# A third pass of seven half-size products in the first of two MLPs, on one Trainium2 core

## The chip, the core and the metric

The kernel runs on one core of a Trainium2 chip. The metric is device time of one execution in microseconds; the kernel before takes 1666.81 us, the median of three runs (1665.36 to 1667.01). Engines in the rows: PE is the matrix engine (TensorE), PEld its weight loads, DVE the vector engine, ACT the activation engine, POOL GpSimd, SP the queue that issues all DMAs here.

## What is computed

Attention over pooled keys and values for 8 batches of 576 tokens with 8 heads of 64, then two MLPs of 512 x 2048 x 512 over all 4608 tokens:

```python
def _attn_ref(q, k, v):                      # [8, 8, 576, 64]
    k_p = k.reshape(B, H, Sp, 8, D).mean(axis=3)
    v_p = v.reshape(B, H, Sp, 8, D).mean(axis=3)
    scores = scale * np.matmul(q, k_p.transpose(0, 1, 3, 2))
    ...                                      # softmax over 72 pooled keys
    return np.matmul(attn, v_p)
def _moe_ref(x, w_in, w_out):                # 4608 x 512, 512 x 2048, 2048 x 512
    h = x @ w_in
    return np.maximum(0.01 * h, h) @ w_out
def _moe2_ref(x, w_in, w_out):
    r = np.maximum(x @ w_in, 0.0)
    return (r * r) @ w_out
```

The weights arrive as 64-bit floats, which the kernel turns into 32-bit ones itself ("decoding").

## The kernel before

Every product in 32-bit precision is made of three matmuls (`three`, lines 271 to 276): each operand is split into a rounded part `hi` and a rest `lo` (a cast on ACT, a subtraction on DVE), and hi hi, hi lo and lo hi are accumulated.

The first MLP treats its 4608 tokens in two ways. The first 3072 go in six **plain tiles** of 512 tokens. A unit is one tile `t` and one 128-wide slice `f` of the 2048 hidden columns (16 to a tile): `first` makes 12 matmuls into `h`, applies the leaky ramp and splits the result into `gh` and `gl`; `second` makes 12 matmuls into four accumulators. The weights stay in SBUF in full and are split again for each unit by `split_weights` (two casts and two subtractions of 128 x 512). The remaining 1536 tokens go in two **passes** of 768 (`LEAD` = 2): `first2` and `second2` compute a 2 x 2 block product with seven half-size products in place of eight, with blocks of 384 tokens (`HT`). A pass is 56 steps ("hooks") of 12 matmuls of 384 columns; each needs one weight block of 512 KB, loaded from DRAM by `next_block` through a ring of six buffers, five of them ahead. The second MLP is six passes of the same make over all tokens, whose `second2` has 18 matmuls of 256 columns a hook.

The blocks of the first MLP come from two places: the plain halves are stored by `split_weights` in tile `NTILE - 2` (line 190) and the sums of halves by `prepare_sums`. The blocks of the second MLP come from `prepare_products` (lines 237 to 269): for each of 8 slice pairs and for `in` and `out` it loads 1 MB, decodes, forms four sums, splits all into `hl` (one buffer) and stores 768 KB and 1 MB. It is a generator; each `next` is a step, 8 steps for an `in` block and 9 for an `out` block, 136 in all.

Order: everything is traced in the order of the loop at line 908, and the framework then orders each engine's instructions by that order and by readiness. The loop hands out attention steps (`advance`: 3 a unit in tile 0, 5 later, `RATES`), then one step of `prepare_sums` a unit, and once attention is through, three steps of `prepare_products` a unit (line 941). In the second half of the last tile the pools of the passes are opened over the space of the early weights (lines 944 to 956) and `products_x(0)` splits the operands of the first pass, one of seven a unit. In the passes (line 972) every second hook is given one step of `prepare_products` until they are used up. Stores are put off by some ticks (`later`, `tick`) so that SP does not wait for the data.

Of the kernel before, what the change touches and what calls it, by code (L numbers as in the profile page):

```python
# [8 lines left out]
F32 = mybir.dt.float32  # L9
F32R = mybir.dt.float32r  # L10
# [7 lines left out]
P = 128  # L18
POOL = 8
KM = 64  # L20
TT = 512
# [6 lines left out]
def raw(ap):  # L28

    return ap.bitcast(F32)  # L30
# [3 lines left out]
def attention_two_mlps(  # L34
# [12 lines left out]
    B, H, S, D = q.shape  # L47
    NT, DM = out.shape
# [10 lines left out]
    AHEAD = 5  # L59
    RATES = (3, 5)  # L60
    HT = 384
    NTILE = 6
    NPASS = NT // (2 * HT)
    PLAIN = NTILE * TT
    LEAD = (NT - PLAIN) // (2 * HT)
    NQ = NF // 2
    HD = DM // 2
    RING = 6
# [3 lines left out]
    dpool = ctx.enter_context(tc.tile_pool(name="dram", bufs=1, space=DRAM))  # L72
# [3 lines left out]
    xpool = one_stack.enter_context(tc.tile_pool(name="x", bufs=5))  # L76
    gpool = one_stack.enter_context(tc.tile_pool(name="g", bufs=2))
# [4 lines left out]
    ps_a = one_stack.enter_context(tc.tile_pool(name="ps_a", bufs=4, space=PSUM))  # L82
# [4 lines left out]
    def temp(name, dt=F32):  # L87
        return tpool.tile([P, TT], dt, tag="t", name=name)

    def work(name, n=TT, early=False):  # L90
        if early:
            return ps_a.tile([P, n], F32, tag="acc", name=name)
        return ps_w.tile([P, n], F32, tag="w", name=name)
# [5 lines left out]
    nc.scalar.activation(warm, ident[:, 0:1], AF.Exp)  # L99


    x0 = [dpool.tile([DM, TT], F32, name=f"x0_{t}") for t in range(NTILE)]
    x0 += [dpool.tile([DM, HT], F32, name=f"x0_{NTILE + t}") for t in range(2 * LEAD)]
    x1 = [dpool.tile([DM, HT], F32, name=f"x1_{t}") for t in range(NT // HT)]

# [5 lines left out]
    def place(g):  # L111

        if g < PLAIN:
            return g // TT, g % TT, TT
        return NTILE + (g - PLAIN) // HT, (g - PLAIN) % HT, HT


# [3 lines left out]
    def later(n, **kw):  # L121
        LATE.append([n, kw])
# [59 lines left out]
    def split_weights(kind, t, f):  # L182

        w = W[kind, f]
        hl = hlpool.tile([P, 2, TT], F32R, tag="hl", name=f"hl_{kind}_{t}_{f}")
        hi, lo = hl[:, 0], hl[:, 1]
        nc.scalar.copy(hi, w)
        nc.vector.tensor_tensor(out=lo, in0=w, in1=raw(hi), op=ALU.subtract)  # L188
        HL[kind, t, f] = (hi, lo)
        if t == NTILE - 2:  # L190
            p, i = f % NQ, f // NQ
            for j in range(2):
                part = {(0, 0): 0, (0, 1): 1, (1, 1): 2}.get((i, j) if kind == "in" else (j, i))
                if part is not None:
                    later(
                        2, out=WD[1, kind, p // 2][part, :, p % 2].rearrange("p (h x) -> p h x", h=2),
                        in_=raw(hl)[:, :, j * HD:(j + 1) * HD],
                    )
# [404 lines left out]
    ready = [0]  # L603
# [10 lines left out]

    def new_x(t):
        X[1, t] = [
            tuple(xpool.tile([P, TT], F32R, tag=g, name=f"{g}1_{t}_{c}") for g in ("xh", "xl"))
            for c in range(NK)
        ]

    def load_x(t):
        XS[t] = []
        for c in range(NK):
            st = temp(f"xs1_{t}_{c}")
            nc.sync.dma_start(out=st, in_=x0[t][c * P:(c + 1) * P, :])
            XS[t].append(st)

# [9 lines left out]
    def first(t, f):  # L637

        x = X[1, t]
        wh, wl = HL.pop(("in", t, f))  # L640
        h = work(f"h1_{t}_{f}")
        for c in range(NK):
            cs = slice(c * P, (c + 1) * P)
            three(h, (wh[:, cs], wl[:, cs]), x[c], c == 0, c == NK - 1)
        g = temp(f"g1_{t}_{f}")
        nc.scalar.activation(g, h, AF.Prelu, alpha=0.01)
        gh = gpool.tile([P, TT], F32R, tag="gh", name=f"gh1_{t}_{f}")
        gl = gpool.tile([P, TT], F32R, tag="gl", name=f"gl1_{t}_{f}")
        nc.scalar.copy(gh, g)  # L649
        nc.vector.tensor_tensor(out=gl, in0=g, in1=raw(gh), op=ALU.subtract)  # L650
        G[t, f] = (gh, gl)

    A = {}

    def store_x1(t, j, o):
        at = t * TT
        while at < (t + 1) * TT:
            n = min((t + 1) * TT, (at // HT + 1) * HT) - at
            nc.sync.dma_start(
                out=x1[at // HT][j * P:(j + 1) * P, at % HT:at % HT + n], in_=o[:, at - t * TT:at - t * TT + n]  # L660
            )
            at += n

    def second(t, f):
        gh, gl = G.pop((t, f))
        wh, wl = HL.pop(("out", t, f))
        if f == 0:
            A[t] = [ps_a.tile([P, TT], F32, tag="acc", name=f"acc1_{t}_{j}") for j in range(4)]
        acc = A[t]
        for j in range(4):  # L670
            js = slice(j * P, (j + 1) * P)
            three(acc[j], (wh[:, js], wl[:, js]), (gh, gl), f == 0, f == NF - 1)
        if f == NF - 1:
            for j in range(4):
                o = temp(f"o1_{t}_{j}")
                if j % 2 == 0:
                    nc.scalar.copy(o, acc[j])
                else:
                    nc.vector.tensor_copy(o, acc[j])
                store_x1(t, j, o)  # L680
# [6 lines left out]
    def load_x2(t):  # L687
        XS2[t] = []
        for j in range(2):
            src = x0[NTILE + 2 * t + j] if t < LEAD else x1[2 * (t - LEAD) + j]  # L690
            st = x2pool.tile([P, NK, HT], F32, tag=f"xs{j}", name=f"xs2_{t}_{j}")
# [10 lines left out]
    def products_x(t):  # L702
# [21 lines left out]
    uses = [  # L724
        (1 if t < LEAD else 2, kind, a, prod)
        for t in range(LEAD + NPASS)
        for kind, a, prod in [("in", a, o[1]) for a in range(NQ // 2) for o in ORDER]
# [81 lines left out]
    def second2(t):  # L809
        banks = {}  # L810
        shape = [P, 2, HT] if t < LEAD else [P, 3, HD]
        s1, s2, s5 = (tmpool.tile(shape, F32, tag=f"s{i}", name=f"so{i}_{t}") for i in (1, 2, 5))
        stores = []
        xg = products_x(t + 1) if t + 1 < LEAD + NPASS else iter(())
        for k, (i, prod) in enumerate(ORDER):
# [35 lines left out]
            else:  # L851
# [7 lines left out]
                if t < LEAD:  # L859
                    dst = x1[PLAIN // HT + 2 * t + n][d * HD:(d + 1) * HD, :].rearrange("(u p) x -> p u x", p=P)  # L860
                else:
# [31 lines left out]
    prep, preparing, hooks = None, True, 0  # L893
# [13 lines left out]
    x2pool, xg = None, iter(())  # L907
    for i, (t, f) in enumerate(units):
        if f == NF - 3 and t + 1 < NTILE:
            while ready[0] * S < min((t + 2) * TT, NT):  # L910
                advance()
            put_stores(made)
            load_x(t + 1)
        if f == NF - 1 and t + 1 < NTILE:
            split_x(t + 1)

        rate = RATES[min(t, 1)]
        if i + 1 < len(units):
            first(*units[i + 1])
        tick()  # L920
        if i + 2 < len(units):
            split_weights("in", *units[i + 2])
        if i + 1 < len(units):
            split_weights("out", *units[i + 1])
        while at_work and made < due + rate // 2:
            advance()
        second(t, f)
        tick()
        due += rate
        while at_work and made < due:  # L930
            advance()
        if w1 < NF:
            prepare_weights(w1)
            w1 += 1
        elif t > 0:
            next(sums1, None)
        if not at_work:
            if prep is None:
                ppool = ctx.enter_context(tc.tile_pool(name="prep", bufs=1, side="right", reuse_waits="tile"))
                prep = prepare_products()  # L940
            for _ in range(3):
                if preparing and next(sums1, 1) and next(prep, 1):
                    preparing = False
        if t == NTILE - 1 and f >= NQ:
            if x2pool is None:
                assert not at_work and next(sums1, 1)
                w_early_stack.close()
                x2pool = ctx.enter_context(tc.tile_pool(name="x2", bufs=1, side="right", reuse_waits="tile"))
                ring = ctx.enter_context(tc.tile_pool(name="ring", bufs=RING, side="right", reuse_waits="tile"))
                load_x2(0)  # L950
                tick(9)
                blocks.insert(0, next_block())
            else:
                if not XO:
                    xg = products_x(0)
                next(xg, None)
# [7 lines left out]
    for t in range(LEAD + NPASS):  # L964
        lead[0] = t < LEAD
        for half in (first2, second2):
            if half is second2 and t + 1 < LEAD + NPASS:
                load_x2(t + 1)
            for _ in half(t):
                tick()  # L970
                hooks += 1
                if hooks % 2 == 0 and preparing and next(prep, 1):
                    preparing = False
                    tick(9)

# [28 lines left out]
```

## Time and profile before

| | |
|---|---|
| median of three runs | 1666.81 us |
| the profiled execution | 1667.88 us |
| its span, first to last instruction | 1666.1 us |
| PE busy | 1615.4 us, 97% |
| DVE busy | 1219.9 us, 73% |
| ACT busy | 858.3 us, 52% |
| DMA moved | 403.88 MB, mean 242 GB/s |
| plain tiles end, passes begin | 723.04 us |
| second MLP begins | 956.00 us |

Busy is the union of an engine's instructions; overlapping matmuls are counted once, and a matmul's duration (0.39 us at 512 columns) is longer than the distance to the next one (0.227 us). So the pace is read from counts in a window, and idle time from the difference between a window's length and PE's busy time.

### The profile page before, as it was taken

How to read it: one execution, taken by the hardware profiler on the slowest of the kernel's cores; microseconds unless marked ns; L12 is line 12 of the kernel's file. 1: busy time of each engine (PE TensorE's matmuls, PEld its weight loads, DVE VectorE, ACT ScalarE, POOL GpSimd, SP SyncE). 2: the span in 40 equal slices, each digit the busy share in tenths (PEclk: the TensorE clock that was granted, in tenths of full speed). 3: DMA queues.
4: the chain of work that ended last, by engine and by line, in shares of the span. 5: the costliest groups of instructions: out<-in, count | busy, mean ns of one | idle time of the engine just before them, and what ended most of it. 6: DMA issues, size and time to landing. Idle time of an engine off the chain costs nothing.

```text
span 1666.1 us, 26276 instructions
## 1 busy us (share of the span) xinstructions
PE 1615.4 (97%) x9688; PEld 1496.2 (90%) x9688; DVE 1219.9 (73%) x1795; ACT 858.3 (52%) x1527; POOL 132.5 (8%) x149
## 2 busy tenths in 40 slices
PE   4899999999999999999999999999999999999998
PEld 3677778778888888889999999999999999999998
DVE  5899999998778778967628459378477487485484
ACT  5788766655666666756435325334234244244233
POOL 3132223322210000000000000000000000000000
PEclk7799999999999999999999999999999999999999
DMA  7565666663326987979878878978878879878776
GB/s 179 184 197 173 187 195 201 196 216 85 95 92 228 307 303 242 319 278 311 294 273 286 287 258 272 305 254 286 293 249 297 281 251 302 277 247 272 269 253 203
DMA packets 215808, 403.88 MB, mean 242 GB/s; under 512 B 55424, under 2 KB 119936, under 8 KB 215680
## 3 DMA queue, kind: packets, MB, share of 16 engines
q1 hardware_dynamic: 215680, 402.19, 73.5%
q8 instruction: 78, 1.28, 0.3%
q14 instruction: 50, 0.41, 0.1%
HBM read 314.57 MB, written 85.98 MB: 240 GB/s over the span
## 4 chain that ended last, share of the span: by engine, by line
PE 77%; DVE 14%; ACT 3%; DMA 3%; issue 2%; SPq 1%; POOL 0%; DVEq 0%; ACTq 0%; POOLq 0%
PE acc L276 12%; PE h L274 12%; PE acc L275 12%; PE acc L274 12%; PE h L275 12%; PE h L276 12%; DVE gl L650 1%; DVE hl_out L188 1%; PE s L470 1%; DVE hl_in L188 1%; DVE v L313 1%; DMA st_in_out<-in_moe_w_out_dram 1%; DVE mx L478 1%; ACT x L481 1%; DMA xs<-x 1%
## 5 line engine op out<-in xcount | busy, mean ns | idle before, releaser
L696 ACT CAST oh<-g 128x768 fp32r<-128x768 f32 x224 | 187.2, 836 | 283.8 <-PE acc L275 165.1
L275 PE MATMUL h<-xl,wb_in 128*128 128x384 f32 x896 | 299.3, 334 | 0.0
L274 PE MATMUL h<-xh,wb_in 128*128 128x384 f32 x896 | 299.3, 334 | 0.0
L276 PE MATMUL h<-xh,wb_in 128*128 128x384 f32 x896 | 299.3, 334 | 0.0
L697 DVE TENSOR_TENSOR ol<-g,oh 128x768 fp32r<-128x768 f32 x224 | 213.6, 954 | 102.1 <-ACT oh L696 101.3
L276 PE MATMUL acc<-wb_out,ol 128*128 128x256 f32 x1008 | 282.2, 280 | 0.0
L274 PE MATMUL acc<-wb_out,oh 128*128 128x256 f32 x1008 | 281.2, 279 | 0.0
L275 PE MATMUL acc<-wb_out,oh 128*128 128x256 f32 x1008 | 281.2, 279 | 0.0
L275 PEld LDWEIGHTS acc<-wb_out,oh 128*128 128x128 f32 x1008 | 189.5, 188 | 0.0
L276 PEld LDWEIGHTS acc<-wb_out,ol 128*128 128x128 f32 x1008 | 189.2, 188 | 0.0
L274 PEld LDWEIGHTS acc<-wb_out,oh 128*128 128x128 f32 x1008 | 188.5, 187 | 0.0
L791 DVE TENSOR_TENSOR g<-h,s 128x768 f32<-128x768 f32 x32 | 30.6, 956 | 191.7 <-PE h L276 112.2
L275 PEld LDWEIGHTS h<-xl,wb_in 128*128 128x128 f32 x896 | 168.2, 188 | 0.0
L274 PEld LDWEIGHTS h<-xh,wb_in 128*128 128x128 f32 x896 | 168.2, 188 | 0.0
L276 PEld LDWEIGHTS h<-xh,wb_in 128*128 128x128 f32 x896 | 168.2, 188 | 0.0
L274 PE MATMUL h<-xh,hl_in 128*128 128x512 f32 x384 | 153.4, 400 | 4.4 <-DVE x L486 2.2
L274 PE MATMUL acc<-gh,hl_out 128*128 128x512 f32 x384 | 153.7, 402 | 0.7 <-ACT gh L649 0.7
L275 PE MATMUL acc<-gl,hl_out 128*128 128x512 f32 x384 | 150.8, 393 | 1.3 <-DVE gl L650 1.3
L276 PE MATMUL acc<-gh,hl_out 128*128 128x512 f32 x384 | 150.9, 393 | 1.1 <-DVE hl_out L188 1.1
L276 PE MATMUL h<-xh,hl_in 128*128 128x512 f32 x384 | 150.4, 392 | 0.0
L275 PE MATMUL h<-xl,hl_in 128*128 128x512 f32 x384 | 150.0, 391 | 0.0
L700 DVE TENSOR_TENSOR g<-g,g 128x768 f32<-128x768 f32 x128 | 120.7, 954 | 6.1 <-ACT g L758 4.6
(148 smaller groups left out, 2976.9 us busy)
## 6 DMA issues: line engine op xcount, KB each, us to landing
wb_in<-wd_in SPq DMA_DIRECT2D x224, 512.0 KB, 4.4
wb_out<-wd_out SPq DMA_DIRECT2D x224, 512.0 KB, 4.5
xs<-x SPq DMA_DIRECT2D x16, 768.0 KB, 7.1
out_dram<-o SPq DMA_DIRECT2D x24, 384.0 KB, 3.9
k<-in_k_dram SPq DMA_DIRECT2D x64, 128.0 KB, 2.9
q<-in_q_dram SPq DMA_DIRECT2D x32, 256.0 KB, 4.0
st_in_out<-in_moe_w_in_dram SPq DMA_DIRECT2D x16, 512.0 KB, 4.1
st_in_out<-in_moe_w_out_dram SPq DMA_DIRECT2D x16, 512.0 KB, 5.6
```

The lines of the kernel that those rows point to most:

```text
L188: nc.vector.tensor_tensor(out=lo, in0=w, in1=raw(hi), op=ALU.subtract)
L274: nc.tensor.matmul(outp, ah, bh, start=first, stop=False, **kw)
L275: nc.tensor.matmul(outp, ah, bl, start=False, stop=False, **kw)
L276: nc.tensor.matmul(outp, al, bh, start=False, stop=last, **kw)
L313: nc.vector.tensor_tensor(out=dst if n == D else src[:, :, 0:n], in0=src[:, :, 0:n], in1=src[:, :, n:2 * n], op=ALU.add)
L470: nc.tensor.matmul(sc[:n, 2 * m:2 * m + 2].rearrange("p a x -> p (a x)"), qT[:, 2 * e + m, :n], kT[b % 2][:, 2 * e + m].rearrange("p a x - ...
L478: nc.vector.tensor_reduce(out=mx[:n], in_=sc[:n], axis=AX.X, op=ALU.max, negate=True)
L481: nc.scalar.activation(x[:n, 4 * e + h], sc[:n, h], AF.Exp, bias=mx[:n, h], accum_out=sm[:n, 4 * e + h],)
L696: nc.scalar.copy(hi, src)
L697: nc.vector.tensor_tensor(out=lo, in0=src, in1=raw(hi), op=ALU.subtract)
L700: nc.vector.tensor_tensor(out=out_, in0=a, in1=b, op=ALU.subtract)
L791: nc.vector.tensor_tensor(out=g11, in0=v, in1=s1, op=ALU.add)
```

## The change

`LEAD` is set to 3, so a third pass takes 768 further tokens, and the plain part shrinks from 3072 to 2304 tokens: four tiles of 512 and a fifth of 256 (`WIDE`). Everything of a plain tile is cut to its width. The stores of the plain halves of the first weights are made in tile `NTILE - 3` = 2 (before: 4). `prepare_products` gets three steps a unit beside a full tile, one a unit in the first six units of the short tile and none in the rest, and beside the passes two of three hooks (before: one of two). The pools of the passes are opened at unit 6 of the last tile (before: 8).

```diff
-    NTILE = 6
+    LEAD = 3
     NPASS = NT // (2 * HT)
-    PLAIN = NTILE * TT
-    LEAD = (NT - PLAIN) // (2 * HT)
+    PLAIN = NT - LEAD * 2 * HT
+    WIDE = [min(TT, PLAIN - at) for at in range(0, PLAIN, TT)]
+    NTILE = len(WIDE)
...
-            return g // TT, g % TT, TT
+            return g // TT, g % TT, WIDE[g // TT]
...
-        if t == NTILE - 2:
+        if t == NTILE - 3:
...
+        n = WIDE[t]
+        h = work(f"h1_{t}_{f}")[:, :n]
...
-        while at < (t + 1) * TT:
-            n = min((t + 1) * TT, (at // HT + 1) * HT) - at
+        end = at + WIDE[t]
+        while at < end:
+            n = min(end, (at // HT + 1) * HT) - at
...
-            while ready[0] * S < min((t + 2) * TT, NT):
+            while ready[0] * S < min((t + 2) * TT, PLAIN):
...
-            for _ in range(3):
+            for _ in range(3 if WIDE[t] == TT else 1 if f < NQ - 2 else 0):
                 if preparing and next(sums1, 1) and next(prep, 1):
                     preparing = False
-        if t == NTILE - 1 and f >= NQ:
+        if t == NTILE - 1 and f >= NQ - 2:
...
-                if hooks % 2 == 0 and preparing and next(prep, 1):
+                if hooks % 3 and preparing and next(prep, 1):
```

## Rows read from the trace of the kernel before

**Rows 1.** The page: busy time, and the busy tenths in 40 slices.

```profile
PE 1615.4 (97%) x9688; PEld 1496.2 (90%) x9688; DVE 1219.9 (73%) x1795; ACT 858.3 (52%) x1527; POOL 132.5 (8%) x149
...
DVE  5899999998778778967628459378477487485484
...
PEclk7799999999999999999999999999999999999999
```

**Rows 2.** The chain that ended last, in order: start us, us, what.

```profile
669.61 8.05 DMA xs<-x
...
719.68 0.69 DVE gl L650
1661.81 0.80 ACT o L854
```

**Rows 3.** Windows: us, busy (instructions) by engine, PEclk, DMA share, GB/s.

```profile
560.00:630.00 70.00, 70.00 (x311) 57.96 (x310) 54.97 (x89) 47.37 (x78) 0.00 (x0) 1.00 0.91 312
845.00:895.00 50.00, 50.00 (x291) 50.00 (x290) 24.81 (x27) 25.36 (x32) 0.00 (x0) 1.00 0.76 257
1020.00:1070.00 50.00, 50.00 (x427) 50.00 (x426) 33.98 (x38) 21.14 (x26) 0.00 (x0) 1.00 0.89 297
```

**Rows 4.** Windows at the stage borders; columns as in rows 3.

```profile
350.00:440.00 90.00, 88.61 (x479) 73.88 (x477) 71.44 (x140) 52.79 (x110) 22.84 (x29) 1.00 0.43 127
549.00:680.00 131.00, 131.00 (x579) 108.47 (x579) 104.38 (x167) 86.61 (x144) 0.00 (x0) 1.00 0.85 288
680.00:723.00 43.00, 41.63 (x183) 33.92 (x182) 42.53 (x66) 31.46 (x51) 0.00 (x0) 1.00 0.77 270
723.04:839.52 116.48, 116.48 (x674) 116.48 (x672) 71.08 (x81) 57.09 (x73) 0.00 (x0) 1.00 0.90 310
839.52:956.00 116.48, 116.48 (x673) 116.48 (x673) 64.72 (x70) 54.18 (x67) 0.00 (x0) 1.00 0.83 280
```

**Rows 5.** Whom PE waited for, 549 to 723 us: total us, times, longest.

```profile
PE acc L274 <- ACT gh L649: 0.7, 1, 0.7
PE acc L275 <- DVE gl L650: 0.6, 1, 0.6
```

**Rows 6.** Groups of `prepare_products`, 475 to 760 us: count, busy, mean ns, idle before.

```profile
L162 DVE SCALAR_TENSOR_TENSOR wm_out<-st_out_out,wm_out 128x1024 uint32<-128x1024 uint32 x8 | 9.8, 1222 | 0.1
L155 DVE TENSOR_SCALAR wm_out<-wm_out 128x1024 f32<-128x1024 f32 x8 | 5.5, 688 | 0.1
L203 DVE TENSOR_TENSOR ops_in<-ops_in 128x256 f32<-128x256 f32 x8 | 3.4, 419 | 0.1
L261 DVE TENSOR_TENSOR hl_out<-ops_out,hl_out 128x1024 fp32r<-128x1024 f32 x8 | 9.8, 1225 | 9.4 <-ACT hl_out L260 9.4
L153 ACT ACTIVATE wm_out<-st_out_out 128x1024 f32<-128x1024 f32 x8 | 9.2, 1153 | 2.7 <-DVE ops_in L172 2.7
L260 ACT CAST hl_in<-ops_in 128x1024 fp32r<-128x1024 f32 x8 | 8.4, 1054 | 7.4 <-DMA wd_in<-hl_in 6.2 <-DVE hl_in L188 1.2
L260 ACT CAST hl_out<-ops_out 128x1024 fp32r<-128x1024 f32 x8 | 8.4, 1050 | 6.1 <-DMA wd_out<-hl_out 4.4 <-DVE hl_out L188 1.5
L260 ACT CAST hl_in<-ops_in 128x512 fp32r<-128x512 f32 x8 | 5.0, 621 | 3.7 <-DMA wd_out<-hl_out 3.2 <-DVE ops_in L172 0.4
```

**Rows 7.** Groups of a plain unit and of `products_x`; columns as in rows 6.

```profile
L188 DVE TENSOR_TENSOR hl_out<-w,hl_out 128x512 fp32r<-128x512 f32 x43 | 29.5, 687 | 6.4 <-ACT hl_out L187 6.3
L697 DVE TENSOR_TENSOR xl<-xs,xh 128x768 fp32r<-128x768 f32 x7 | 6.6, 952 | 1.9 <-ACT xh L696 1.9
```

**Rows 8.** An ACT copy in the first pass; SP's longest wait, 723 to 781 us.

```profile
727.40 0.80 ACT L787 COPY s<-h 128x768 f32<-128x768 f32 x1 [1.28 <-PE h L276]
...
SPq L129 <- DVE hl_in L261: 3.1, 1, 3.1
```

**Rows 9.** DMA: a window as in rows 3; GB/s in 40 slices of 723 to 781 us.

```profile
730.00:770.00 40.00, 40.00 (x232) 40.00 (x231) 22.63 (x28) 22.32 (x30) 0.00 (x0) 1.00 0.94 343
...
GB/s 226 295 301 319 285 393 421 285 356 223 398 412 407 427 410 339 206 260 328 153 258 405 418 294 384 299 357 210 356 412 424 407 240 322 277 263 223 288 266 223
```

More of the change, by code (lines that the diff above doesn't have):

```diff
@@ L99, in attention_two_mlps @@
     nc.scalar.activation(warm, ident[:, 0:1], AF.Exp)
-    x0 = [dpool.tile([DM, TT], F32, name=f"x0_{t}") for t in range(NTILE)]
+    x0 = [dpool.tile([DM, WIDE[t]], F32, name=f"x0_{t}") for t in range(NTILE)]
     x0 += [dpool.tile([DM, HT], F32, name=f"x0_{NTILE + t}") for t in range(2 * LEAD)]
@@ L616, in new_x @@
         X[1, t] = [
-            tuple(xpool.tile([P, TT], F32R, tag=g, name=f"{g}1_{t}_{c}") for g in ("xh", "xl"))
+            tuple(xpool.tile([P, TT], F32R, tag=g, name=f"{g}1_{t}_{c}")[:, :WIDE[t]] for g in ("xh", "xl"))
             for c in range(NK)
@@ L623, in load_x @@
         for c in range(NK):
-            st = temp(f"xs1_{t}_{c}")
+            st = temp(f"xs1_{t}_{c}")[:, :WIDE[t]]
             nc.sync.dma_start(out=st, in_=x0[t][c * P:(c + 1) * P, :])
@@ L640, in first @@
         wh, wl = HL.pop(("in", t, f))
-        h = work(f"h1_{t}_{f}")
+        n = WIDE[t]
+        h = work(f"h1_{t}_{f}")[:, :n]
         for c in range(NK):
@@ L644, in first @@
             three(h, (wh[:, cs], wl[:, cs]), x[c], c == 0, c == NK - 1)
-        g = temp(f"g1_{t}_{f}")
+        g = temp(f"g1_{t}_{f}")[:, :n]
         nc.scalar.activation(g, h, AF.Prelu, alpha=0.01)
-        gh = gpool.tile([P, TT], F32R, tag="gh", name=f"gh1_{t}_{f}")
-        gl = gpool.tile([P, TT], F32R, tag="gl", name=f"gl1_{t}_{f}")
+        gh = gpool.tile([P, TT], F32R, tag="gh", name=f"gh1_{t}_{f}")[:, :n]
+        gl = gpool.tile([P, TT], F32R, tag="gl", name=f"gl1_{t}_{f}")[:, :n]
         nc.scalar.copy(gh, g)
@@ L667, in second @@
         if f == 0:
-            A[t] = [ps_a.tile([P, TT], F32, tag="acc", name=f"acc1_{t}_{j}") for j in range(4)]
+            A[t] = [ps_a.tile([P, TT], F32, tag="acc", name=f"acc1_{t}_{j}")[:, :WIDE[t]] for j in range(4)]
         acc = A[t]
@@ L674, in second @@
             for j in range(4):
-                o = temp(f"o1_{t}_{j}")
+                o = temp(f"o1_{t}_{j}")[:, :WIDE[t]]
                 if j % 2 == 0:
```

## The prediction, made before the change was run

> **What bounds the kernel now.** I read the page first: TensorE is busy 97% of the span, at the full granted clock in all but the first two of 40 slices, and the vector engine is at 9 tenths in the first third, then at 3 to 8 [rows 1]. So there are two regimes. The chain of waits shows where they meet: its last piece away from TensorE before a long stretch of matmuls alone is a subtraction for a plain tile at 719.68 us, and the next is the last copy out at 1661.81 us [rows 2]. I then cut the trace into windows at the stage borders. From 549 to 723 us (the last two plain tiles) TensorE is busy in all but 1.4 us; from 723.04 to 956.00 us (the two half-size passes of the first MLP) it has no gap at all, each pass taking 116.48 us [rows 4]. The list of who TensorE waited for in the two tiles has two entries, 0.7 and 0.6 us, both at the chain piece above [rows 5]. Behind the attention the time is therefore a count of matmuls times their pace, as long as nothing else comes late. The vector engine is the second limit: 99% busy in the last 43 us of the plain tiles [rows 4]. DMA is the third: 0.90 busy at 310 GB/s in the first pass and 0.83 at 280 in the second [rows 4].
>
> **The pace of a matmul.** Counts in three clean windows [rows 3], less about two matmuls cut by the edges: 512 columns 70/309 = 0.2265 us, 384 columns 50/289 = 0.173, 256 columns 50/425 = 0.1177. Halving 512 does not halve the time; the half tile pays 4% more per token.
>
> **Removed.** Two plain tiles of 16 x 24 = 384 matmuls: 768 x 0.2265 = 174.0 us, and the 1.4 us of idle in them. **Added.** One tile of 256 tokens, 384 x 0.1177 = 45.2 us, and a third pass, 116.5 us [rows 4]. On TensorE alone: -175.4 + 161.7 = **-13.7 us**. All else is what the new arrangement uncovers.
>
> The Trainium skill, "TensorE: Matmul & The Clock Gate", section "Back-to-back issue gap", gives N/2.4 + 2.5 ns, so 216, 162.5 and 109 ns here. By it the sum would be -165.9 + 41.9 + 109.2 = -14.8 us before idle; the rows show 9 to 11 ns more per matmul and I go by them.
>
> **The short tile.** Its weights are still split at full width, so other engines keep most of their work while TensorE has half. The vector engine, in durations: 32 weight splits x 0.69 = 22.0, 16 `gl` of 256 columns at 0.42 (any 128x256 row) = 6.7, `x` splits 1.7, copies out 2.2, six steps of second-weight work 5.6 (0.93 each, below), and `products_x(0)`, seven splits and four differences at 0.95 = 10.5 [rows 6, 7]. Sum 48.7 us; successive starts lie up to 0.08 us closer than the durations, which takes off some 4: 44.6 to 48.7, against 45.2 of TensorE. It is full. The nearest stretch, 680 to 723 us, has the vector engine full as well and costs 1.4 us of TensorE in 43 [rows 4]. I take 3 us, between 0 (work of `products_x` slides) and 8 (the long sum plus one wait of 0.3 a unit). The activation engine is nearly as full: 32 weight casts at 0.62 (a 128x512 cast [rows 6]) = 20, ramps and casts of 256 columns at 0.41 = 13, `x` splits, copies, six steps and seven casts of `products_x` 12: 45 us. The 3 us are for both.
>
> **The second weights beside the passes.** `prepare_products` has 17 steps for a pair of blocks, 136 in all. Attention has 34 steps a batch and gets 3 a unit in tile 0, then 5: it ends in tile 3, unit 5. Before, 43 units follow at 3 steps: 129 steps, and 7 are left to the first pass. After, 11 units at 3 and 6 at 1: 39 steps, and 97 go to the passes, two in three hooks, the last at hook 146 of 168. A hook is 116.48/56 = 2.08 us, so this lasts 304 us.
> - Vector engine: a block costs two scalings at 0.69, a merge at 1.222, an add at 1.222 (in two halves of 0.69 for `out`), four sums at 0.42 and subtractions of 1.225 + 0.69 + 0.42 [rows 6]; a pair 15.8 us, 0.93 a step. A pass gets 37 steps, 34.7 us, on 64.7 already there [rows 4]: 99.4 of 116.5, 85%. Hidden. ACT: 8.95 us a pair, 0.53 a step, 19.7 + 54.2 = 74, 63%. Hidden.
> - Blocking: ACT and the vector engine take their instructions in the order written. TensorE needs ACT's copy of one product about one hook later; ACT idles 1.28 us there [rows 8], and a piece of this work lasts up to 1.22 us. In the first pass of before seven such steps run without a gap on TensorE. Its casts also wait for the store of the one `hl` buffer, 13.8 us in the whole run [rows 6]. ACT standing behind such a wait delays the copy of a product. I take 1 us; bounds 0 and 8 (24 stores moved x 0.3).
> - SP: each moved step takes its loads and stores past the block loads on one queue. SP's longest wait for such a store in the first half of pass 0 was 3.1 us [rows 8]; five blocks ahead are 10.4 us of cover. Nothing, unless DMA falls behind.
> - DMA: 12.6 MB of the 46.1 MB (16 blocks of 1.05 in and 1.84 out) stay in the tiles, 33.5 go beside the passes: 33.5 MB / 304 us = 110 GB/s, on the 280 of an undisturbed pass: **390 GB/s**. Never sustained in this trace. Nearest: 730 to 770 us, 343 GB/s at 0.94 with no gap on TensorE [rows 9]. For 7 us in it, five slices of 1.45 us in a row, 398 to 427 [rows 9], so the engines can do some 410 for a while. I take 2 us; bounds 0 (410) and 21 (343/0.94 = 365 GB/s; 390/365 stretches 304 us by 6.8%).
>
> **The rest.** Stores of the plain half of the first weights move from tile 4 to tile 2, where the vector engine bounds and DMA is at 0.43 [rows 4]: 48 DMAs of 256 KB, 12.6 MB in some 130 us, about 97 GB/s more. They are issued two ticks after the split, and a `hl` buffer comes round a unit later; nothing, at worst 2 us. `x2pool` opens ten units before the end in place of eight, but these units are half as long: 10 x 24 x 0.1177 = 28 us of lead, not 8 x 24 x 0.2265 = 43. The load that the chain shows there took 8.05 us [rows 2] and seven units of `products_x` follow, 20 us; together just 28, which is why the short tile's 3 us is not smaller. Widths in `place` and `store_x1` cost nothing of their own.
>
> **Sum.** -13.7 + 3 + 1 + 2 = -7.7 us on a profiled execution of 1667.88 us (span 1666.1), which stands 1.1 us above the median. 1666.8 - 7.7 = 1659, and I give 1660, since unknowns here only cost.
>
> **Rivals.**
> - DMA becomes the bound of the passes (slower). For: 390 against 343 seen. Against: 410 in bursts. It decides where the engines sustain less than 390 with this mix of block loads, weight loads and stores; at 365 it costs 21 in place of 2: **1679**. The scheduler may also pull the steps together, which raises the demand while it lasts. Beside it stands a rule of the Trainium skill, "DMA: Bandwidth & Descriptors", section "Specifications": HBM gives a core about 358 GB/s (the fabric 435). By it 390/358 would add 27 us, 1684 in all. The 40 us at 343 agree with it; the slices above 398 don't, for 7 us.
> - The short tile is bound by the vector and activation engines and its chain (copy out, cast, subtract) rather than TensorE: 10 to 12 in place of 3: **1668**, no change. For: 44.6 to 48.7 of 45.2. Against: weight splits run a unit ahead.
> - In-order ACT behind late stores. Each of 24 stores costs 0.7 in place of 0.04: +16, **1675**. For: 1.28 us of slack per product. Against: the first pass shows none.
> - The change doesn't do what it says: the scheduler orders by readiness, so the steps stay close to the tiles, the short tile takes them as well and lengthens by two blocks of vector work, 16 us: **1675**.
>
> **Chances.** Forecast 0.50, DMA 0.22, short tile 0.14, ACT 0.08, not as said 0.06. A measurement of this kernel tells about 0.2% (3.3 us) from none: faster is under 1663.5, slower over 1670. The forecast's own range, 1653 to 1665, is nearly all faster; the short tile mostly lands within; of DMA's 0.22 about 0.04 is mild enough to land within. Faster 0.48, same 0.19, slower 0.33. The range 1653 to 1680 takes in both bounds of the three costs but not their worst together.
>
> **What would show it.** A third stretch of 116.5 us with TensorE busy throughout; the short tile 45 to 50 us; DMA share near 1.0 at 370 to 400 GB/s until late in the third pass. Passes of 118 to 125 us with gaps before matmuls that read `wb_in` or `wb_out`, waiting for DMA, are the first rival; gaps waiting for copies `s` or casts `oh`, the third. If tile 3 or the attention ends later than before, the moved stores were not free and the prediction fails on that side.

## The result, and the profile after

The changed kernel takes **1677.3 us** (median of four runs, 1675.7 to 1679.5), the kernel before 1666.2 us in the same runs: a ratio of 1.0069 (95% interval 1.0057 to 1.0082). It is 0.7% slower; 1660.0 and a gain had been forecast.

The page of the changed kernel, two lines that answer to [rows 1]:

```profile
span 1676.4 us, 26986 instructions
PE 1612.2 (96%) x9976; PEld 1519.3 (91%) x9976; DVE 1241.4 (74%) x1811; ACT 863.1 (51%) x1524; POOL 132.4 (8%) x149
```

TensorE is busy 3 us less than in [rows 1], yet the span is 10 us longer: some 13 us of idle were added. To place them I cut the trace at the short tile, at the six halves of the three passes, and at the first half of the second MLP; the last window is one of some ten matmuls after a gap. Windows of the changed kernel: us, busy (instructions) of PE, PEld, DVE, ACT, POOL, PEclk, DMA share, GB/s.

```profile
546.00:594.86 48.86, 48.17 (x383) 46.80 (x382) 47.11 (x80) 40.29 (x83) 0.00 (x0) 1.00 0.74 262
594.86:653.21 58.35, 58.35 (x339) 58.20 (x337) 43.49 (x61) 35.74 (x47) 0.00 (x0) 1.00 0.94 328
653.21:711.44 58.23, 58.23 (x337) 58.23 (x337) 44.59 (x54) 28.71 (x37) 0.00 (x0) 1.00 0.94 331
711.44:777.29 65.85, 61.97 (x338) 61.33 (x338) 30.60 (x37) 31.56 (x39) 0.00 (x0) 0.95 0.90 310
777.29:837.88 60.59, 59.40 (x337) 58.82 (x337) 55.62 (x71) 35.60 (x46) 0.00 (x0) 1.00 0.95 341
837.88:903.35 65.47, 59.50 (x338) 58.10 (x337) 37.62 (x52) 35.58 (x46) 0.00 (x0) 1.00 0.95 347
903.35:966.17 62.82, 60.60 (x337) 60.07 (x337) 45.60 (x52) 28.85 (x36) 0.00 (x0) 0.97 0.86 315
966.17:1024.40 58.23, 58.23 (x337) 58.23 (x337) 37.94 (x42) 20.82 (x26) 0.00 (x0) 1.00 0.83 288
774.20:777.20 3.00, 3.00 (x11) 3.00 (x10) 3.00 (x4) 1.00 (x2) 0.00 (x0) 0.50 1.04 406
```

The short tile takes 48 to 49 us, nearly all TensorE. Pass 0 takes 116.6 us, as the passes of [rows 4]. Passes 1 and 2 take 126.4 and 128.3: **21.8 us more than two undisturbed ones**, and nothing is lost after 966 us. The loss has two main parts. In eight gaps of 0.3 to 2.6 us TensorE is idle for 13.3 us; some 5 us are three stretches behind gaps, as in the last row, in which the granted clock is at its lower level (0.50, 1.2 instead of 2.4 GHz) and matmuls of 384 columns start up to 0.32 us apart instead of 0.173. The rest lies in smaller delays, most of them right behind the gaps.

Who was late in these passes, 594.86 to 966.17 us (us in total, times, longest; SyncE's queue and ScalarE below TensorE):

```profile
PE h L275 <- DMA wb_in<-wd_in: 6.0, 4, 2.6
PE acc L275 <- DMA wb_out<-wd_out: 3.4, 2, 2.2
PE h L275 <- DVE g L798: 2.0, 1, 2.0
PE h L275 <- ACT s L788: 1.9, 1, 1.9
...
SPq L130 <- DVE hl_out L262: 20.6, 4, 7.8
SPq L130 <- DVE hl_in L262: 10.6, 2, 6.0
...
ACT wm_out L154 <- DMA st_out_out<-in_moe_w_out_dram: 7.0, 2, 4.6
ACT hl_in L261 <- DMA wd_in<-hl_in: 6.2, 5, 2.0
```

Six gaps end on a block load, 9.4 us in all. In these passes SyncE stood six times, 31 us in all, at the store of a step (line 130, `hl`), with block loads behind it; in [rows 8] its longest such wait was 3.1 us. Two gaps, 3.9 us, end instead on a product's copy (line 788) and a product's sum (line 798), which stood behind ScalarE's wait for a weight load. One of each kind, from the timelines of SyncE, ACT, DVE and PE (start, us, what, idle before and its end):

```profile
857.15 1.25 SPq L740 DMA_DIRECT2D wb_in<-wd_in  x1
864.47 0.37 SPq L130 DMA_DIRECT2D wd_out<-hl_out  x1
864.93 17.19 SPq L740 DMA_DIRECT2D wb_in<-wd_in  x11
...
861.43 1.05 ACT L261 CAST hl_out<-ops_out 128x1024 fp32r<-128x1024 f32 x1 [0.43 <-DMA wd_out<-hl_out]
...
862.35 0.96 DVE L794 TENSOR_TENSOR g<-h,s 128x768 f32<-128x768 f32 x1 [6.64 <-PE h L277]
863.22 1.22 DVE L262 TENSOR_TENSOR hl_out<-ops_out,hl_out 128x1024 fp32r<-128x1024 f32 x1
...
871.12 0.41 PE L275 MATMUL h<-xh,wb_in 128*128 128x384 f32 x1 [2.64 <-DMA wb_in<-wd_in]
...
770.76 1.12 ACT L154 ACTIVATE wm_out<-st_out_out 128x1024 f32<-128x1024 f32 x1 [4.65 <-DMA st_out_out<-in_moe_w_out_dram]
...
771.92 0.69 DVE L156 TENSOR_SCALAR wm_out<-wm_out 128x1024 f32<-128x1024 f32 x1 [3.50 <-ACT wm_out L154]
772.53 0.95 DVE L798 TENSOR_TENSOR g<-h,s 128x768 f32<-128x768 f32 x1
```

At 858.4 us SyncE reaches a store whose data VectorE is to write at line 262. The cast that line 262 needs (line 261) has its place on ScalarE behind copies of products and waits for the buffer's store before it; it ends at 862.48. Line 262 stands behind line 794 besides, which waits 6.64 us for TensorE's next product. So the store goes out at 864.47, block loads follow at once, the first of them is the block that TensorE needs next, and TensorE waits for it until 871.12. In the other four gaps of over 0.5 us that end on a block, too, the late block is the first behind a store that waited; the first and the last of the five:

```profile
807.38 0.37 SPq L130 DMA_DIRECT2D wd_out<-hl_out  x1
807.84 4.00 SPq L740 DMA_DIRECT2D wb_out<-wd_out  x5
...
814.68 0.41 PE L275 MATMUL acc<-oh,wb_out 128*128 128x384 f32 x1 [1.19 <-DMA wb_out<-wd_out]
...
926.46 0.37 SPq L130 DMA_DIRECT2D wd_out<-hl_out  x1
926.92 4.31 SPq L740 DMA_DIRECT2D wb_out<-wd_out  x6
...
933.10 0.42 PE L275 MATMUL acc<-oh,wb_out 128*128 128x384 f32 x1 [2.22 <-DMA wb_out<-wd_out]
```

All five were issued only 6.2 to 6.8 us before their use, where the blocks of a pass without steps (e1, below) are issued 10.2 us before. Only one other block was late, by 0.3 us. At 770.76 ScalarE has waited 4.65 us for a weight load; VectorE stands behind it, and its line 798, which TensorE needs, starts late.

Two readings were open. **Bandwidth**: DMA can't carry the steps' traffic beside the block loads. **Order**: it could, but waits in in-order queues hold block loads and product copies back.

### The profile page after: what moved, and what is told of

Same layout as the page of the kernel before. It is cut to its first block, busy times and chain, and to the rows that moved or that the text cites. A ratio compares the mean times of both kernels' runs of the same rounds, so it can differ in the third digit from the quotient of the medians.

```text
span 1676.4 us, 26986 instructions
## 1 busy us (share of the span) xinstructions
PE 1612.2 (96%) x9976; PEld 1519.3 (91%) x9976; DVE 1241.4 (74%) x1811; ACT 863.1 (51%) x1524; POOL 132.4 (8%) x149
## 4 chain that ended last, share of the span: by engine, by line
PE 70%; DVE 17%; DMA 5%; ACT 3%; issue 3%; SPq 1%; POOL 0%; DVEq 0%; ACTq 0%; POOLq 0%
PE h L275 12%; PE h L276 12%; PE h L277 12%; PE acc L277 11%; PE acc L276 11%; PE acc L275 11%; DVE hl_out L189 1%; DMA wb_in<-wd_in 1%; DVE ol L700 1%; DVE hl_in L189 1%; DVE gl L652 1%; PE s L471 1%; DMA st_in_out<-in_moe_w_out_dram 1%; DVE mx L479 1%; DVE v L314 1%
## 5 line engine op out<-in xcount | busy, mean ns | idle before, releaser
L699 ACT CAST oh<-g 128x768 fp32r<-128x768 f32 x252 | 210.1, 835 | 281.4 <-PE acc L276 165.1
L275 PE MATMUL h<-xh,wb_in 128*128 128x384 f32 x1008 | 339.1, 336 | 9.8 <-DMA wb_in<-wd_in 6.0
L276 PE MATMUL h<-xl,wb_in 128*128 128x384 f32 x1008 | 338.5, 336 | 0.0
L277 PE MATMUL h<-xh,wb_in 128*128 128x384 f32 x1008 | 338.3, 336 | 0.0
L700 DVE TENSOR_TENSOR ol<-g,oh 128x768 fp32r<-128x768 f32 x252 | 240.3, 955 | 90.4 <-ACT oh L699 89.9
L275 PEld LDWEIGHTS h<-xh,wb_in 128*128 128x128 f32 x1008 | 190.2, 189 | 12.0 <-issue 3.8
L277 PEld LDWEIGHTS h<-xh,wb_in 128*128 128x128 f32 x1008 | 190.4, 189 | 0.0
L276 PEld LDWEIGHTS h<-xl,wb_in 128*128 128x128 f32 x1008 | 190.3, 189 | 0.0
L275 PE MATMUL h<-xh,hl_in 128*128 128x512 f32 (+1 forms) x320 | 121.9, 382 | 4.3 <-DVE x L487 2.1
L275 PE MATMUL acc<-gh,hl_out 128*128 128x512 f32 (+1 forms) x320 | 120.2, 383 | 0.8 <-ACT gh L651 0.8
L276 PE MATMUL acc<-gl,hl_out 128*128 128x512 f32 (+1 forms) x320 | 118.7, 372 | 1.2 <-DVE gl L652 1.1
L277 PE MATMUL acc<-gh,hl_out 128*128 128x512 f32 (+1 forms) x320 | 118.6, 372 | 1.0 <-DVE hl_out L189 1.0
L277 PE MATMUL h<-xh,hl_in 128*128 128x512 f32 (+1 forms) x320 | 118.7, 371 | 0.0
L276 PE MATMUL h<-xl,hl_in 128*128 128x512 f32 (+1 forms) x320 | 118.5, 370 | 0.0
```

Source lines behind the costliest of these rows:

```text
L275: nc.tensor.matmul(outp, ah, bh, start=first, stop=False, **kw)
L276: nc.tensor.matmul(outp, ah, bl, start=False, stop=False, **kw)
L277: nc.tensor.matmul(outp, al, bh, start=False, stop=last, **kw)
L699: nc.scalar.copy(hi, src)
L700: nc.vector.tensor_tensor(out=lo, in0=src, in1=raw(hi), op=ALU.subtract)
```

## Experiments: what the parts cost alone

**e1, no steps beside the passes.** The 97 steps are left out; the second MLP loads the first one's blocks, as many bytes, here and in e3, e5 and e6.

```diff
-                if hooks % 3 and preparing and next(prep, 1):
+                preparing = False
```

> The changed kernel without the 97 steps of prepare_products beside the passes (left out: the second weights are decoded only in part, and the second MLP reads the blocks of the first). It prices everything that these steps do. If the loss lies in the passes alone, as the windows after say (126.4 and 128.3 us in place of 116.5), all three passes take 116.5 and the kernel 1677.3 - 21.8 = 1655.5 us (1653 to 1658). If the third pass or the short tile is slow of itself, it stays above 1660. Both theories below expect 1655.5.

Measured 1653.9 us, ratio 0.9916 (0.9901 to 0.9931). Each of the three passes takes 116.5 us; the first:

```profile
592.50:708.98 116.48, 116.48 (x674) 116.48 (x673) 65.15 (x71) 53.59 (x67) 0.00 (x0) 1.00 0.86 279
```

So the trade on TensorE, short tile included, is worth 13.8 us against the kernel before (1667.7 in these runs), and the steps cost some 23.4. The kernel before measured 1666.2 to 1667.7 us from one set of runs to the next, so differences across sets carry some 1.5 us.

**e6, the steps' work on the engines alone,** without their loads and stores; **e5, their traffic alone,** issued by SyncE at the steps' places. In e5:

```diff
+                if hooks % 3 and hooks <= 146:
+                    steps += 1
+                    p, kind, at = (2 + steps // 14) % NQ, ("in", "out")[steps % 14 > 6], steps % 14 % 7
+                    if at == 0:
+                        fetch_weights(2, [(kind, p), (kind, p + NQ)])
+                    elif at in (3, 5):
...
```

> The engine work by itself: all 97 steps decode, sum, cast and subtract beside the passes, but from the third pair's second block on nothing is loaded or stored for them (the second MLP reads the blocks of the first). Theory C (engines: 1.2 us pieces on ACT and the vector engine block the copies that TensorE waits for): 1662 to 1670. Theories A and B: the pieces fit, 1654 to 1658 us.

> The transfers by themselves: as e1 (no steps beside the passes, the second MLP reads the blocks of the first), but SP issues loads of second weights that nobody reads and stores of a constant buffer, at the places of the steps, some 32 MB in all, so about the 390 GB/s of the changed kernel; nothing waits for them and they wait for no engine. Theory B (bandwidth): the passes lengthen as in the changed kernel, 1672 to 1680 us. Theory A (order: waits of stores, casts and decodes in the queues): passes near 116.5, 1654 to 1658.

e6: 1655.4 us (ratio 0.9931, 0.9917 to 0.9946), 1.5 over e1, though without transfers to wait for the steps crowd into pass 0. e5: 1665.8 us (0.9994, 0.9984 to 1.0003), **11.9 over e1**. Pass 0 of e6, then windows of e5:

```profile
594.86:711.44 116.58, 116.38 (x670) 115.55 (x669) 113.82 (x157) 81.47 (x107) 0.00 (x0) 1.00 0.87 281
...
594.86:711.44 116.58, 116.58 (x674) 116.58 (x673) 64.73 (x70) 54.04 (x67) 0.00 (x0) 1.00 0.96 333
770.00:830.00 60.00, 56.77 (x327) 56.19 (x326) 40.43 (x45) 26.09 (x33) 0.00 (x0) 1.00 1.01 382
830.00:890.00 60.00, 56.34 (x315) 55.74 (x314) 17.92 (x19) 23.21 (x29) 0.00 (x0) 0.97 0.98 361
...
770.38 13.93 SPq L740 DMA_DIRECT2D wb_out<-wd_out  x7
...
781.65 0.41 PE L275 MATMUL acc<-oh,wb_out 128*128 128x384 f32 x1 [2.26 <-DMA wb_out<-wd_out]
```

VectorE can be 98% busy beside a pass at little cost to TensorE (0.9 us in e6's pass 0). Traffic can't: e5 loses nothing at 333 GB/s and loses once the share reaches 0.98 to 1.01, with no work of the steps on any engine. Its four late blocks were issued 9.5 to 12.4 us before their use (6.2 to 6.8 in the changed kernel) and landed too late all the same, one of them in the last two lines. This is bandwidth, though not purely: once, at 831.8 us, SyncE had stood 5.8 us at a store of the first MLP's own output (line 870), 19 us ahead of e5's longest gap.

1677.3 less 1653.9, 1.5 and 11.9 leaves **10 us that only both together cost**. But e5 is not the changed kernel's traffic: it spends 14 steps on a pair of blocks where the generator takes 17, and its three passes moved 125.0 MB where the changed kernel's moved 122.0 and e1's 97.8. Its second and third pass moved 42.6 and 43.8 MB and lost 3.7 and 7.4 us; the changed kernel's moved 41.1 and 42.5 and lost 10.0 and 11.8. So 11.9 is probably too much for the changed kernel's bytes and 10 too little for what order adds.

**e3, stores of a quarter of the bytes.** Every step and store stays in the code, in its place.

```diff
-  out=WD[2, kind, p // 2][at:at + n, :, p % 2]..., in_=raw(hl)[:, :n]...
+  out=WD[2, kind, p // 2][at:at + n, :, p % 2, 0:128]..., in_=raw(hl)[:, :n]...[:, :, 0:128]
```

> The stores of prepare_products stay on SP with their waits and order, but carry a quarter of the bytes (the rest of each row is not stored; the second MLP reads the blocks of the first): demand beside the passes falls from 390 to some 338 GB/s, less than the 343 of before. Theory B: no gaps, 1655 to 1659 us. Theory A: the SP holds stay, 1668 to 1677; at best the hl buffer comes free sooner, which takes some of ACT's waits away.

1662.0 us (0.9965, 0.9952 to 0.9978): 15.3 back. No gap ends on a block load any more; 3.6 us are left behind ScalarE's copies (lines 788, 792). But e3 does not tell the readings apart: no store of a step held SyncE for more than 3.2 us (7.8 in the changed kernel), so the waits went with the bytes, and the steps closed up (line 154 runs 5, 2 and 0 times in its three passes; 2, 4 and 2 times in the changed kernel's).

## Experiments: freeing a queue or a buffer

**e4, a ring of seven blocks** (`RING = 7`) for longer cover.

> RING is 7: six blocks ahead in place of five, 2.08 us more cover, same bytes. Theory A: the five gaps that end on a block load (1.0 to 2.8 us each) shrink to about a third, 1668 to 1672 us. Theory B: an even shortage is not helped by a deeper ring, 1675 to 1679.

1679.0 us (1.0070, 1.0054 to 1.0087): no change. SyncE's waits at line 130 grew to 27.1 and 13.9 us, the longest 10.7 (20.6, 10.6 and 7.8 in the changed kernel), which is more than the 2.08 us of cover that the ring gained.

**e2, stores from GpSimd's queue, at once; e7, two `hl` buffers** of three quarters the size, with three stores a block in place of two; **e8, both.**

```diff
-                    later(3, out=WD[2, ...
+                    nc.gpsimd.dma_start(out=WD[2, ...                      # e2, e8
-  hl = ppool.tile([P, 4, 2, HD], ...)
+  hl = ppool.tile([P, 3, 2, HD], ..., bufs=2)                             # e7, e8
```

> The stores of prepare_products go out on GpSimd's queue at once, not on SP behind a delay; bytes, casts and decodes are unchanged. Theory A (order: a store that waits for its data holds SP, and the block loads behind it come late): the gaps that end on wb loads go, some 9 to 11 us, 1666 to 1669 us, and the gaps that end on copies and casts stay. Theory B (bandwidth: 390 GB/s is more than the DMA engines give): the passes stay at 126 to 128 us, 1675 to 1680.

> Same bytes as the changed kernel, but the pieces to be stored have two buffers of three parts in place of one of four (pieces of 3, 2 and 2 parts), so a cast no longer waits for the store just before, and a store's data is ready earlier. Theory A: most of the gaps go, 1656 to 1666 us. Theory B: unchanged, 1674 to 1680.

> As e7, and the stores go out at once on GpSimd's queue as in e2. In e2 the casts stood 60 us in all behind stores of the one buffer; with two buffers these waits should mostly go. Theory A: 1655 to 1668. Theory B: 1675 or more; e2's 1702 again if the steps are pulled together and the transfers bunch.

1702.3 us (1.0202, 1.0187 to 1.0218), 1683.9 (1.0099, 1.0084 to 1.0115) and 1692.0 (1.0158, 1.0141 to 1.0175): all slower. **e15 moves the block loads** of the first MLP to GpSimd's queue instead, so that none stands behind a store; e16 does so on the spread kernel below.

```diff
-            nc.sync.dma_start(out=raw(w), in_=WD[layer, kind, a][PART[prod]])
+            queue = nc.gpsimd if layer == 1 else nc.sync
+            queue.dma_start(out=raw(w), in_=WD[layer, kind, a][PART[prod]])
```

> The changed kernel with the block loads of the first MLP's passes issued from GpSimd's queue in place of SyncE's; GpSimd has no other work in the passes. Same bytes, same steps, same stores on SyncE. No block load then stands behind a store that waits for VectorE (waits of up to 7.8 us in the changed kernel). If these waits turn the short transfers into the loss: gaps on wb_in and wb_out go, some 8 to 12 us of the 21.8 in passes 1 and 2, and the time is 1664-1670. If the sum of transfers (353 and 365 GB/s) is the limit by itself: the blocks still land late, 1674-1680. A queue that issues more slowly than SyncE's would show as longer landing times in every pass, pass 0 too.

> The same, on the spread kernel (steps until hook 182, first layer's pairs of blocks first), which moved 334 GB/s without loss in four halves and lost 8.1 us in the second MLP's first half and 5 in the first half of pass 0. The blocks of the second MLP stay on SyncE. If order is what is left: the 0.7 to 1.7 us in pass 2 go, and part of the 8.1 does not (its blocks are on SyncE still): 1666-1669. If GpSimd's queue issues more slowly, over 1672.

1706.5 us (1.0242, 1.0228 to 1.0256) and 1705.1 (1.0231, 1.0217 to 1.0245). No gap ends on a block load, as expected of order, and yet the kernel is slower. Up to 711 us blocks landed in a median of 6.0 to 6.1 us (5.1 to 5.6 in the changed kernel); somewhat later, but since TensorE waited for none of them, this does not explain it. Who waited in e15, 590 to 1030 us, and where its weights were decoded (line 154: busy (count) to 711.44 us, to 816.61 us, and behind):

```profile
PE h L275 <- DVE g L799: 13.8, 5, 5.7
PE acc L275 <- ACT oh L699: 8.3, 3, 4.5
PE h L275 <- ACT s L789: 6.8, 4, 3.5
...
ACT hl_out L261 <- DMA wd_out<-hl_out: 22.3, 5, 8.7
ACT hl_in L261 <- DMA wd_in<-hl_in: 18.7, 5, 6.4
ACT hl_in L261 <- DMA wd_out<-hl_out: 13.2, 4, 5.8
ACT hl_out L261 <- DMA wd_in<-hl_in: 10.2, 4, 3.4
...
594.86:711.44 116.58, 4.64 (x4) 0.96 0.95 333
711.44:816.61 105.17, 4.59 (x4) 0.95 0.91 320
816.61:990.00 173.39, 0.00 (x0) 1.00 0.89 293
```

The three halves to 816 us take 71, 75 and 74 us, then nothing is lost. The order in which the scheduler puts the instructions when the kernel is built has changed with the queue, and the steps close up: line 154 runs 5, 3 and 0 times in e15's own three passes, 2, 4 and 2 times in the changed kernel's. Then the casts of line 261 stand 64 us in all on ScalarE for the store of the `hl` buffer, and product copies stand behind them. e2 shows the same (60 us of such waits, nothing lost behind 812 us), e8 too (52 us, 806). So in the changed kernel the queue on which stores and block loads alternate seems also to have paced the steps; that it is the cause is argued, and it is not the only one, since e3's steps closed up with both on SyncE.

## Experiments: the same bytes, placed otherwise

**e9, a group's load four steps earlier; e10, three steps in five hooks; e11, both; e12,** e11 with four steps a unit in the last wide tile and five steps in nine hooks.

```diff
                 sums(ops[:, 4:8], *(ops[:, i] for i in range(4)))
+                fetch_group(n + 1)                                     # e9, e11, e12
-                if hooks % 3 and preparing and next(prep, 1):
+                if hooks % 5 in (1, 3, 0) and preparing and ...        # e10, e11
```

> The changed kernel with the load of the next group of second-MLP weights issued four steps earlier (beside the sums of the group before), everything else as it is: the same bytes, the same 97 steps at the same pace. In the changed kernel two of the gaps of TensorE began with ScalarE waiting 2.3 and 4.6 us for such a load with a product copy behind it. If that in-order wait is what turns the transfers (12 us alone) into the whole loss (23 us): ScalarE no longer waits for st_in/st_out, and the time falls by 5 to 10 us, to 1667-1672. If the loss is bandwidth throughout, the same bytes in the same time cost the same: 1675-1679, with gaps that end on block loads (wb_in, wb_out).

> The changed kernel with the steps at three of five hooks instead of two of three, so that the same 97 steps and the same bytes end just ahead of the second MLP (some 162 hooks of 168 instead of 146). If the bandwidth of the moment is the limit, the traffic of the steps falls by a tenth (32 MB over some 338 us instead of 304), the sum of demand comes to about 347 GB/s, near what was carried without loss in the kernel before (338), and the time falls by 6 to 12 us, to 1665-1671. If the loss hangs on each wait in a queue instead, there are as many waits as before and it stays at 1674-1679.

> Both edits: the earlier load of each group and three steps in five hooks. If bandwidth and the in-order waits are two causes whose losses add, this takes the sum of the two single gains, 10 to 20 us, and ends at 1657-1667, perhaps under the kernel before (1666.8). If one is only the other's sign, it gives what the better of the two gives.

> As the run with both edits, and four steps instead of three beside each unit of the last 512-token tile, so that some 7 of the 97 steps go there, and five steps in nine hooks for the rest. The tile's window has VectorE busy 41.3 of 46.8 us, a step costs it some 1.3 us, so up to 5 us of cover are there for 7 steps at 9 us: the tile may grow by 0 to 4 us. The passes' traffic falls by another 7 %. If the bandwidth of the moment decides: passes 1 and 2 keep 58.24 us a half, and the time is 1654-1662. If not: as the run with both edits, plus what the tile grows.

1675.2 us (1.0048, 1.0035 to 1.0061), 1676.5 (1.0060, 1.0047 to 1.0072), **1670.6** (1.0025, 1.0016 to 1.0034) and 1671.4 (1.0027, 1.0016 to 1.0039). Neither edit does much alone; together they give 6.7 us. The seven steps that e12 was to move into the tile did not lighten the passes: 121.9 MB in its three against 120.6 in e11's, and the tile took 104.9 us in both. e9 did not take the waits away (line 154 still stood 4.9 and 3.3 us for such loads). e10's expectation missed because the slower pace only shifted the load: its passes moved 38.4, 39.4 and 43.0 MB and lost 1.4, 7.8 and 14.3 us, where the changed kernel lost 0.1, 10.0 and 11.8. The megabytes of the three passes of the changed kernel:

```profile
DMA packets 13215, 38.45 MB, mean 330 GB/s; under 512 B 1132, under 2 KB 2924, under 8 KB 13205
DMA packets 15407, 41.12 MB, mean 325 GB/s; under 512 B 1156, under 2 KB 4996, under 8 KB 15399
DMA packets 15151, 42.47 MB, mean 331 GB/s; under 512 B 1227, under 2 KB 4555, under 8 KB 15142
```

Over the 116.5 us of an undisturbed pass these would be 330, 353 and 365 GB/s. Some 330 was carried in each, and only pass 0, which asked for no more, lost nothing. But 330 is no ceiling: e5 carried 354 GB/s over its second pass and over its third.

**e13, spread:** all pairs of blocks of the first layer first, then those of the second, which are needed a half pass later, at 8 of 15 hooks, until hook 182; **e14** with the earlier load as well.

```diff
-        for p in range(NQ):
-            for kind in ("in", "out"):
+        for kind in ("in", "out"):
+            for p in range(NQ):
-                if hooks % 3 and preparing and next(prep, 1):
+                if hooks * 8 % 15 < 8 and preparing and next(prep, 1):
```

> The changed kernel with the groups of second-MLP weights in another order (all eight pairs of blocks of the first layer, then all eight of the second, which is needed one half pass later) and the steps at 8 of 15 hooks, so that they go on until hook 182, 14 hooks into the second MLP. The same bytes and steps; loads and waits as in the changed kernel. In the changed kernel the three passes moved 38.5, 41.1 and 42.5 MB, that is 330, 353 and 365 GB/s if each had taken 116.5 us, and only the first lost nothing. If the sum of transfers is the limit: some 10 % less in each of the last two passes brings them to 335-345 GB/s, most of their 21.8 us goes, the second MLP's first half (288 GB/s before) takes the rest, and the time is 1656-1666. If it is the order of the waits: as many waits as before, 1672-1679.

> The same spread, and the load of each group issued four steps earlier. If the sum of transfers is the limit and the waits only add to it where it is short: little on top of the spread alone, 1654-1664. If the waits are a cause of their own: the same 2 to 6 us under the run with the spread alone that the earlier load gave before (1677.3 to 1675.2 at one pace, 1676.5 to 1670.6 at the other).

1670.0 us (1.0021, 1.0011 to 1.0030) and 1671.5 (1.0034, 1.0022 to 1.0046). In e13's windows (two halves of passes, the next two, the last half of pass 2, and the second MLP's first half):

```profile
657.36:773.84 116.48, 116.48 (x673) 116.48 (x673) 76.98 (x94) 60.14 (x79) 0.00 (x0) 1.00 0.95 329
773.84:890.99 117.15, 116.96 (x674) 116.37 (x673) 77.79 (x98) 61.60 (x81) 0.00 (x0) 1.00 0.94 333
890.99:950.93 59.94, 58.67 (x337) 58.38 (x337) 50.47 (x63) 32.59 (x42) 0.00 (x0) 1.00 0.95 338
950.93:1017.27 66.34, 60.79 (x337) 60.18 (x337) 43.14 (x51) 22.73 (x29) 0.00 (x0) 0.95 0.90 316
```

At 329 to 333 GB/s, with 24 to 28 instructions a pass on VectorE and 12 to 14 on ScalarE over e1's 70 and 67, 233.6 us pass with 0.7 us lost. In this stretch SyncE stood at the store of a step only once, 2.1 us, so it shows that traffic at this rate fits, and not what a long wait in the queue would have cost beside it. What e13 still loses lies at its ends: 5.0 us in the first half of pass 0, mostly behind a late sum on VectorE and the lower clock after it; 1.7 in the third row, where the late block was again the first behind a store; and 8.1 in the last row, where SyncE stood 6.7 us at a store of `hl_out`, block loads left at once, TensorE waited 4.5 us and then ran at the lower clock. There DMA moved 316 GB/s at 0.90: this one is order. e14 shows that the earlier load adds nothing to the spread.

No version that does all the work beat the kernel before. The nearest, e13 and e11, stand 0.2% above it.

## Why the prediction was wrong

- **TensorE's sum: right.** -13.7 and 3 for the short tile, -10.7 in all; e1 gives -13.8. The short tile took 48.2 us where 48 were told, 2 us of it the steps that moved there (46.2 in e1). Three passes alone run without a gap.
- **Moved stores of the first weights: right.** The plain tiles end within 2 us of where they did, earlier rather than later; the new loads of `x2` stalled nobody.
- **The moved transfers, 2 us on DMA and nothing on SyncE: the step that failed.** They and the waits that they bring make up some 20 of the 21.8 us that the passes lost. Both halves were wrong.
- *DMA, 2 us with bounds 0 and 21.* The demand was put at 390 GB/s, too high: the builder's order pulled work ahead (line 154 runs 8 of its 16 times for second weights before 594.86 us), so that 24 MB came beside the passes (122.0 MB, less 97.8 in e1's three) and not 33.5. It was 330, 353 and 365. The capacity was put at some 410, also too high: that rested on five slices of 1.45 us [rows 9]. The 40 us at 343 and 0.94 in the same group were the better row. Over a pass, loads and stores of this mix went without loss at 329 to 333 GB/s (e13, e5's pass 0); the windows of e5 that lost had 361 and 382 at shares of 0.98 and 1.01. Alone, traffic cost 11.9 us in e5, with 3 MB more than the changed kernel's passes moved; so the term was probably worth less.
- *SyncE, "nothing, unless DMA falls behind".* SyncE's wait per store went from 3.1 us to 7.8, and 9.4 of the 13.3 us of idle end on blocks; all but 0.3 us of that on blocks issued right behind such a wait. The prediction set the waits against 10.4 us of cover, but a block also has to land within it. In the changed kernel the median landing was 4.9 to 6.8 us in passes 1 and 2, which leaves 3.6 to 5.5; the five waits that led to gaps were 4.7 to 7.8. Slower landing (4.4 to 4.8 in e1) and longer waits thus add up, which fits the 10 us or more that no single part costs; how much of the 21.8 is bandwidth and how much order the runs don't settle.
- **Blocking, 1 us with bounds 0 and 8: right for the work alone** (1.5 in e6), too small beside the transfers, though within its bounds: two gaps, 3.9 us, and the lower clock behind both, some 3. The bound counted waits on ScalarE for stores; what came was weight loads that were late.
- **The rivals.** "DMA becomes the bound" at 1679 stands next to the 1677.3 measured, and in part by luck: it came with a lower demand and with waits in SyncE's queue that it did not have. The in-order rival was part of it, with SyncE rather than ScalarE behind most of the loss. Its argument "the first pass shows none" was drawn from a pass with room on DMA and with seven steps. The short tile was not it. "Not as said" was half true: the steps did move toward the tile, which grew by 2 us and not 16.
- Of the Trainium skill ("DMA: Bandwidth & Descriptors", "Specifications") the figure of 358 GB/s stood beside the first rival. The traces agree in part: 343 went without loss for 40 us [rows 9], and e5 lost at 361. But e5 also moved 382 GB/s for 60 us, at a share of 1.01, so 358 is no ceiling here; the measurement decides, and by it loss set in between 343 and 361.

## What to carry to other kernels

A term whose bounds are 0 and 21 us, on a change worth 13, is the forecast; take its value from the longest stretch that ran without loss, not from the fastest few microseconds. Beside a stream of block loads, work on idle engines was nearly free here and bytes were not: price the traffic per stretch, at the rate at which it would be asked for if nothing were late. Where one in-order queue carries both the stream and the stores of side work, set a store's longest wait against the ring's cover less the time that a block takes to land. And freeing the queue may change the order of the side work as well.

## What was not expected of the hardware

- Behind three gaps of 1.9 to 2.2 us of idle in the changed kernel, and one of 4.5 us in e13, TensorE ran for some 3 to 5 us at a granted clock near 0.5, though not behind every gap: after the 2.64 us at 871.12 it went on at 0.17 us a matmul. What decides it the runs don't show.
- A DMA share of 0.94 to 0.95 went for 233 us with 0.7 us lost (e13) and 0.98 to 1.01 did not (e5), but the changed kernel lost 21.8 us at 0.86 to 0.95. A pass without steps stands at 0.86 with 279 GB/s (e1), and 343 GB/s, 23% more, at 0.94 [rows 9]: the share does not grow in proportion, and what is left of it is no measure of the traffic that still fits.
